# Sink-window attention and MLP: probabilities transposed on VectorE and by DMAs through DRAM instead of on TensorE, from the third chunk on

## The chip, the core and the metric

The kernel runs on one core of a Trainium2 chip. The metric is the device time of one execution in microseconds (us); of several runs the median is taken. TensorE (PE in the profile) multiplies and transposes into PSUM, VectorE (DVE), ScalarE (ACT) and GpSimd (POOL) compute elementwise, and SyncE (SP) issues the DMAs. All engines run their own queues in order and wait for each other through semaphores.

## The reference

```python
B, H, S, D = 4, 8, 768, 64          # n_sink 4, window 128
scores = (q @ k.T) / sqrt(D)        # per batch and head
keep = (key < n_sink) | ((query - key >= 0) & (query - key < window))
a = softmax(where(keep, scores, -1e9))
x = (a @ v)                         # heads side by side: 3072 x 512
h = maximum(x @ w_in, 0)            # 512 -> 2048
out = (h * h) @ w_out               # 2048 -> 512
```

A query sees the 4 sink keys and the 128 keys up to its own position. All numbers are fp32; the weights, x, and the squares are carried as a high and a low part, so that a product is three matmuls.

## The kernel before

The 3072 tokens are cut into 8 chunks of 384 tokens (half a sequence of one batch; chunk c = 2b + half), and attention for a chunk runs over 4 pairs of heads (p). Queries go in blocks of 128: three per chunk and head. A query block needs at most its own key block and the one before it, and the sinks. Its row of probabilities in P is 264 wide: the earlier key block (columns 0 to 127), 8 sink columns (128 to 135), its own key block (136 to 263). The first block of a sequence (qb = 0) has 128 columns only.

One pair goes through these steps:
- load_qk and load_v (L171, L188) load qn, kn, vn on SP's queue. prep (L211) splits keys and queries into parts KS and QS on DVE, POOL and ACT.
- score (L231): two matmuls into a PSUM bank s of the tag "att" (two banks, shared with pss and pt); DVE adds the mask and takes the minimum (L259); ACT takes the exponential and the sum (L262). After a head's third score normalise (L266) runs: rs and its reciprocal on DVE (L272, L273); POOL adds the two key blocks into columns 0 to 127 (L279), scales (L284), and writes the sink columns to PSK (L290, L293).
- probs_of (L344), once for each head: three TensorE transposes of the added blocks into a bank pt (L353), and DVE multiplies by the 0/1 masks halves that separate the two key blocks again, into PTF (L359, L362, L364). The added blocks hold both: with a window of 128, the earlier block has values above the diagonal only, the own block on and below it.
- sink_keys (L295): transposes PSK into pss (L300) and copies it to SK (L302).
- values (L368): matmuls of vn with PTF and of VS with SK into xo (L384, L387). ACT and DVE split xo into the high and low part of x (L395, L396).

The MLP runs in legs: half of the 2048 hidden features for chunks 0, 1, 0, 1, then all 16 blocks of 128 for each of chunks 2 to 7. One block is 12 matmuls into ph (L442), a ReLU r and a square gh on ACT (L450, L453), the low part gl on DVE (L455, L459), and one block later nine matmuls into the three banks po, one for each block of 128 tokens (L472). At a leg's end evacuate (L484) moves po out through ob (two buffers); for the second half of chunks 0 and 1 it loads the earlier part back (L490) and adds it (L491).

What sets the order: chunks 0 and 1 are written out by hand. From chunk 2 on, a list of units is made for each pair (slot, L415: loads, six scores, the four units of the pair before, two preps), and a plan (L717) spreads the units of the coming chunk evenly over the steps of a leg; within that the tile scheduler orders each engine's queue. The attention of chunk 2 runs beside the MLP of chunks 0 and 1, that of chunk 3 beside chunk 2, and so on; the last leg (chunk 7) has no attention beside it. During the first legs the weights are also loaded (raw, half) and split.

## Time and profile before

| | |
|---|---|
| runs | 718.26, 719.05, 719.45 us, median 719.05 |
| span of the profiled execution | 717.5 us (1.55 below the median) |
| TensorE | 691.0 us, 3866 matmuls and transposes |
| DVE, ACT, POOL | 485.7, 392.4, 232.0 us |
| DMA | 71.78 MB, hardware queue 33.5% of 16 engines |

The span is from the first to the last instruction of the profiled execution. Busy times of different engines overlap; the one near the span is the one whose queue matters. The groups of instructions list busy time, the mean duration of one in ns, and the engine's idle time ahead of them with what ended it. Matmuls follow each other in a pipeline, so that one lasts longer than it holds up the next.

### The profile page before, as it was taken

The page shows a single profiled execution, that of the slowest core. Times are in us where ns is not written, and L with a number is a line of the kernel's source. Part 1 is how long each engine was busy: PE and PEld are TensorE (multiplying, and loading weights), DVE is VectorE, ACT ScalarE, POOL GpSimd, SP SyncE. Part 2 cuts the span into 40 slices and gives each one's busy share as a digit, 9 for nine tenths or more (in the row PEclk, how much of TensorE's full clock was granted, in tenths as well). Part 3 has the DMA queues.
Part 4 walks back from the last instruction along what each step waited for, and adds up shares of the span by engine and source line. Part 5 has one row for each costly group of instructions (what it writes and reads, how often), then busy time and mean ns, then how long its engine had stood idle before and what let it go on. Part 6 is the DMA issues. An engine that isn't in the chain of part 4 may idle for free.

```text
span 717.5 us, 11750 instructions
## 1 busy us (share of the span) xinstructions
PE 691.0 (96%) x3866; PEld 597.4 (83%) x3866; DVE 485.7 (68%) x1278; ACT 392.4 (55%) x1074; POOL 232.0 (32%) x432
## 2 busy tenths in 40 slices
PE   4879999999999999999999999999999999999996
PEld 2557789998878888888988888898888898889995
DVE  6887879996887776666576766766666766543222
ACT  5677666663545665666665665666566444322221
POOL 4552420042454443333244334423342424110000
PEclk9999999999999999999999999999999999999998
DMA  8465356531433522343433433334333310001001
GB/s 238 133 203 167 110 151 211 173 106 46 140 91 80 171 77 73 105 133 94 112 102 90 134 106 93 92 116 122 84 87 103 101 44 15 1 2 45 1 0 49
DMA packets 37013, 71.78 MB, mean 100 GB/s; under 512 B 4368, under 2 KB 14096, under 8 KB 36944
## 3 DMA queue, kind: packets, MB, share of 16 engines
q1 hardware_dynamic: 36944, 70.95, 33.5%
q8 instruction: 33, 0.54, 0.3%
q14 instruction: 36, 0.29, 0.2%
HBM read 63.06 MB, written 7.86 MB: 99 GB/s over the span
## 4 chain that ended last, share of the span: by engine, by line
PE 87%; DVE 6%; POOL 2%; ACT 1%; issue 1%; DMA 1%; SPq 0%; DVEq 0%; POOLq 0%; ACTq 0%
PE ph L442 35%; PE po L472 35%; PE xo L384 5%; PE s L255 4%; PE pt L353 2%; POOL P L284 1%; PE xo L387 1%; PE pss L300 1%; PE pt L335 1%; PE s L251 1%; DVE P L259 1%; ACT P L262 1%; DMA kn<-in_k_dram 1%; DVE ph L455 0%; DVE rs L272 0%
## 5 line engine op out<-in xcount | busy, mean ns | idle before, releaser
L442 PE MATMUL ph<-x,wi 128*128 128x384 f32 x1536 | 307.8, 341 | 0.0
L442 PEld LDWEIGHTS ph<-x,wi 128*128 128x128 f32 x1536 | 265.9, 188 | 8.2 <-issue 1.7
L472 PE MATMUL po<-wo,gh 128*128 128x512 f32 x768 | 243.9, 398 | 0.5 <-DVE ob L491 0.5
L223 POOL TENSOR_TENSOR KS<-kn,KS 128x408 fp32r<-128x408 f32 (+1 forms) x48 | 71.3, 1486 | 325.3 <-DVE KS L222 315.1
L472 PE MATMUL po<-wo,gl 128*128 128x512 f32 x384 | 151.4, 394 | 0.0
L472 PEld LDWEIGHTS po<-wo,gh 128*128 128x128 f32 x768 | 135.8, 188 | 18.6 <-DVE ob L491 0.8
L262 ACT ACTIVATE P<-P,nbs 128x264 f32<-128x264 f32 (+1 forms) x192 | 94.4, 492 | 85.6 <-DVE nbs L259 82.0
L450 ACT ACTIVATE r<-ph 128x384 f32<-128x384 f32 x128 | 62.7, 490 | 109.9 <-PE ph L442 109.0
L455 DVE TENSOR_TENSOR ph<-ph,r 128x384 f32<-128x384 f32 x128 | 71.6, 560 | 66.0 <-ACT r L450 65.3
L284 POOL TENSOR_SCALAR P<-P,rs 128x136 f32<-128x136 f32 (+2 forms) x192 | 82.0, 443 | 43.9 <-DVE rs L273 33.6
L472 PEld LDWEIGHTS po<-wo,gl 128*128 128x128 f32 x384 | 72.0, 188 | 16.0
L259 DVE CUSTOM_DVE_ANT_0 P<-s,maskA 128x264 f32<-128x264 f32 x128 | 53.8, 429 | 45.9 <-PE s L255 43.8
L459 DVE TENSOR_TENSOR gl<-ph,gh 128x384 fp32r<-128x384 f32 x128 | 71.0, 555 | 10.2 <-DVE ph L455 0.5
L453 ACT ACTIVATE gh<-r 128x384 fp32r<-128x384 f32 x128 | 67.1, 524 | 3.5
L255 PE MATMUL s<-KS,QS 128*128 128x264 f32 (+1 forms) x288 | 57.2, 281 | 0.9 <-DVE nbs L259 0.8
L255 PEld LDWEIGHTS s<-KS,QS 128*128 128x128 f32 x288 | 51.7, 188 | 6.6 <-DVE nbs L259 2.2
L359 DVE TENSOR_TENSOR PTF<-pt,halves 128x256 f32<-128x256 f32 x96 | 36.2, 419 | 22.9 <-PE pt L353 22.4
L272 DVE TENSOR_SCALAR rs<-sm 128x3 f32<-128x3 f32 (+1 forms) x56 | 47.3, 844 | 3.1 <-ACT P L262 1.9
L279 POOL TENSOR_TENSOR P<-P 128x256 f32<-128x256 f32 (+1 forms) x48 | 43.3, 902 | 16.7 <-ACT P L262 16.7
L384 PE MATMUL xo<-PTF,vn 128*64 128x256 f32 (+1 forms) x448 | 46.3, 347 | 0.7 <-ACT PTF L342 0.7
L384 PEld LDWEIGHTS xo<-PTF,vn 128*64 128x64 f32 x448 | 28.8, 139 | 21.8 <-issue 10.8
L395 ACT CAST x<-xo 128x384 fp32r<-128x384 f32 x32 | 15.3, 479 | 53.4 <-PE xo L387 53.4
(94 smaller groups left out, 659.9 us busy)
## 6 DMA issues: line engine op xcount, KB each, us to landing
raw<-in_moe_w_in_dram SPq DMA_DIRECT2D x16, 512.0 KB, 5.1
raw<-in_moe_w_out_dram SPq DMA_DIRECT2D x16, 512.0 KB, 3.6
half<-in_moe_w_in_dram SPq DMA_DIRECT2D x32, 256.0 KB, 3.2
half<-in_moe_w_out_dram SPq DMA_DIRECT2D x32, 256.0 KB, 3.2
kn<-in_k_dram SPq DMA_DIRECT2D x24, 272.0 KB, 4.2
qn<-in_q_dram SPq DMA_DIRECT2D x32, 192.0 KB, 3.2
out_dram<-ob SPq DMA_DIRECT2D x24, 256.0 KB, 2.3
kn<-in_k_dram SPq DMA_DIRECT2D x24, 204.0 KB, 3.7
```

The costliest lines, as they stand in the source:

```text
L223: nc.gpsimd.tensor_tensor(KS[:, 1, 0:nk], st["kn"][:, hh, 0:nk], f32(KS[:, 0, 0:nk]), op=ALU.subtract)
L255: nc.tensor.matmul(ps[:, 0:n], st["QS", hh][:, qcols], flat[:, a, c0 : c0 + n], start=(a == 0), stop=(a == 1))
L259: nc.vector.tensor_tensor_reduce(Pt[:, i, 0:n], ps[:, 0:n], mask[:, 0:n], -SCALE, BIG, ALU.add, ALU.min, nb)
L262: nc.scalar.activation(Pt[:, i, 0:n], Pt[:, i, 0:n], AF.Exp, bias=nb, scale=-1.0, accum_out=sm[:, i : i + 1])
L284: nc.gpsimd.tensor_scalar(Pt[:, j, 0:n], Pt[:, j, 0:n], rs[:, hh, j : j + 1], 1.0, op0=ALU.mult, op1=ALU.mult)
L384: nc.tensor.matmul(xo[h * D : h * D + D, cols], lhsT, rhs, start=(n == 0), stop=False, skip_group_check=True)
L442: nc.tensor.matmul(ph[:, 0:TOK], wi_at(i, cc, fc), xt[:, cc, :], start=(m == 0), stop=(m == 3 * NCC - 1),)
L450: nc.scalar.activation(r, ph[:, 0:TOK], AF.Relu)
L453: nc.scalar.activation(gh, r, AF.Square)
L455: nc.vector.tensor_tensor(ph[:, 0:TOK], ph[:, 0:TOK], r, op=ALU.mult)
L459: late = lambda: nc.vector.tensor_tensor(gl, ph[:, 0:TOK], f32(gh), op=ALU.subtract)
L472: nc.tensor.matmul(po[t], gt[:, ts_], wo[f][:, i, :], start=(f == f0 and j == 0), stop=(f == f1 - 1 and j == 2),)
```

## The change

From chunk 2 on, TensorE's transposes of P, the masks halves and POOL's addition are gone. The function turn takes their place: DVE transposes P in blocks of 32x32 into a tile T, once both heads are done four DMAs copy T to a DRAM buffer via, one for each group of 32 partitions, and one DMA loads it back as PT, with the blocks at their transposed places. All key blocks are kept apart, so each query block has two blocks in PT: index i for its own key block (or NQ + i - 1 for the earlier one), and P of qb = 0 is stored at column 136. POOL now scales all 264 columns. values takes its moving operand from PT in four runs of 32 for each 128 columns. P, T and PT have one buffer each (P0 and P1 for the two heads). In slot, the units of the pair before are two, sink_keys behind the first score and values behind the fifth. Before, the third DVE multiply of probs_of stood for the block that only one query block uses; in turn, the third transpose (128x4x32) is issued for the second half of a sequence only.

```diff
@@ -236,7 +226,12 @@
                 st["P"] = []
                 st["sm"] = ap2.tile([P, 2, NQ], F32, tag="sm", name=f"sm_{c}_{p}")
             if i == 0:
-                st["P"].append(ap4.tile([P, NQ, BAND], F32, tag="P", name=f"P_{c}_{p}_{hh}"))
+                if c < 2 and p % 2:
+                    if hh == 0:
+                        both = ap1.tile([P, 2, NQ, BAND], F32, tag="T", name=f"P_{c}_{p}")
+                        st["P"] = [both[:, 0], both[:, 1]]
+                else:
+                    st["P"].append(ap1.tile([P, NQ, BAND], F32, tag=f"P{hh}", name=f"P_{c}_{p}_{hh}"))
             Pt, sm = st["P"][hh], st["sm"][:, hh]
             qb = half * NQ + i
             if qb == 0:
@@ -256,12 +251,16 @@
                         ps[:, 0:n], st["QS", hh][:, qcols], flat[:, a, c0 : c0 + n], start=(a == 0), stop=(a == 1)
                     )
             nb = nbs[:, c * H + 2 * p + hh, i : i + 1]
+            o = BS if c > 1 and qb == 0 else 0
             nc.vector.tensor_tensor_reduce(
-                Pt[:, i, 0:n], ps[:, 0:n], mask[:, 0:n], -SCALE, BIG, ALU.add, ALU.min, nb
+                Pt[:, i, o : o + n], ps[:, 0:n], mask[:, 0:n], -SCALE, BIG, ALU.add, ALU.min, nb
             )
-            nc.scalar.activation(Pt[:, i, 0:n], Pt[:, i, 0:n], AF.Exp, bias=nb, scale=-1.0, accum_out=sm[:, i : i + 1])
+            nc.scalar.activation(
+                Pt[:, i, o : o + n], Pt[:, i, o : o + n], AF.Exp, bias=nb, scale=-1.0, accum_out=sm[:, i : i + 1]
+            )
             if i == NQ - 1 and c * NPAIR + p >= NPS:
                 normalise(c, p, (hh,))
+                turn(c, p, hh)
 
         def normalise(c, p, heads):
             st = state[c, p]
@@ -274,15 +273,11 @@
             for hh in heads:
                 Pt = st["P"][hh]
                 j0 = 1 if half == 0 else 0
-                if c > 1:
-
-                    nc.gpsimd.tensor_tensor(
-                        Pt[:, j0:NQ, 0:P], Pt[:, j0:NQ, 0:P], Pt[:, j0:NQ, BS:BAND], op=ALU.add
-                    )
                 for j in range(NQ):
-                    n = P if j < j0 else (BS if c > 1 else BAND)
+                    n = P if j < j0 else BAND
+                    o = BS if c > 1 and j < j0 else 0
                     nc.gpsimd.tensor_scalar(
-                        Pt[:, j, 0:n], Pt[:, j, 0:n], rs[:, hh, j : j + 1], 1.0, op0=ALU.mult, op1=ALU.mult
+                        Pt[:, j, o : o + n], Pt[:, j, o : o + n], rs[:, hh, j : j + 1], 1.0, op0=ALU.mult, op1=ALU.mult
                     )
                 own = slice(hh * NS, hh * NS + NS)
                 src = Pt[:, i0:NQ, P:BS]
@@ -335,35 +330,43 @@
                     nc.tensor.transpose(
                         pt[:, off + j * P : off + (j + 1) * P], st["P"][hh][:, i, c0 : c0 + P], ident
                     )
-            st["PT"][bi] = PTF = ap3.tile([P, 512], F32, tag="PTF", name=f"PTF_{c}_{p}_{bi}")
+            st["PT"][bi] = PTF = PT.rearrange("p r i h b -> p (r i h b)")[:, bi * 512 : bi * 512 + 512]
             if bi == 1 and c != 1:
                 nc.vector.tensor_copy(PTF[:, 0:used], pt[:, 0:used])
             else:
                 nc.scalar.copy(PTF[:, 0:used], pt[:, 0:used])
 
-        def probs_of(c, p, hh):
+        def turn(c, p, hh):
 
             st = state[c, p]
-            half = c % NHALF
+            j0 = 1 if c % NHALF == 0 else 0
+            Pt = st["P"][hh]
             if hh == 0:
-                st["banks"] = banks_of(c, p)
-                st["PT"] = [ap3.tile([P, 512], F32, tag="PTF", name=f"PTF_{c}_{p}_{bi}") for bi in range(3)]
-            pt = ps_att.tile([P, 512], F32, tag="att", name=f"pt_{c}_{p}_{hh}")
-            for i in range(NQ):
-                nc.tensor.transpose(pt[:, i * P : (i + 1) * P], st["P"][hh][:, i, 0:P], ident)
-            both = lambda t, n: t.rearrange("p (a c) -> p a c", c=n)
-
-            wide = st["PT"][2 * hh].rearrange("p (a t c) -> p a t c", a=2, t=2)
-            for a in range(2):
-                m = halves[:, 0:2] if half == 0 and a == 0 else halves[:, 2:4]
-                nc.vector.tensor_tensor(wide[:, a], both(pt[:, a * P : (a + 2) * P], P), m, op=ALU.mult)
-            thin = both(st["PT"][1], P)
-            if half == 0:
-                nc.vector.tensor_tensor(thin[:, hh], pt[:, 2 * P : 3 * P], halves[:, 2], op=ALU.mult)
-            else:
-                nc.vector.tensor_tensor(
-                    thin[:, hh : 4 : 2], both(pt[:, 0 : 4 * P], P)[:, 0:4:2], halves[:, 1:3], op=ALU.mult
+                st["T"] = ap1.tile([P, 4, 2 * NQ, 2, 32], F32, tag="T", name=f"T_{c}_{p}")
+            T = st["T"]
+            nc.vector.transpose(
+                T[:, :, 0:NQ, hh].rearrange("p c j b -> p j c b"),
+                Pt[:, :, BS:BAND].rearrange("p j (c b) -> p j c b", b=32),
+            )
+            nc.vector.transpose(
+                T[:, :, NQ : 2 * NQ - 1, hh].rearrange("p c j b -> p j c b"),
+                Pt[:, 1:NQ, 0:P].rearrange("p j (c b) -> p j c b", b=32),
+            )
+            if j0 == 0:
+                nc.vector.transpose(T[:, :, 2 * NQ - 1, hh], Pt[:, 0, 0:P].rearrange("p (c b) -> p c b", b=32))
+            if hh == 0:
+                return
+            used = slice(0, 2 * NQ - j0)
+            via = dp.tile([4, 32, 4, 2 * NQ, 2, 32], F32, tag=f"via{p % 2}", name=f"via_{c}_{p}")
+            for r in range(4):
+                nc.sync.dma_start(
+                    out=via[:, :, r, used].rearrange("c a i h b -> a c (i h b)"),
+                    in_=T[32 * r : 32 * r + 32, :, used].rearrange("a c i h b -> a c (i h b)"),
                 )
+            nc.sync.dma_start(
+                out=PT[:, :, used].rearrange("p r i h b -> p r (i h b)"),
+                in_=via[:, :, :, used].rearrange("c a r i h b -> (c a) r (i h b)"),
+            )
 
         def values(c, p, later=False):
 
@@ -373,10 +376,25 @@
             xo = ps_x.tile([P, 512], F32, tag="xo", name=f"xo_{c}_{p}")
             todo = ([], [])
 
-            for bi in (0, 2, 1):
-                for h, kk, qs, off in st["banks"][bi][0]:
-                    n = len(qs) * P
-                    todo[h].append((slice(qs[0] * P, qs[0] * P + n), st["vn"][:, kk, h, :], st["PT"][bi][:, off : off + n]))
+            if c > 1:
+                half = c % NHALF
+                for h in range(2):
+                    blocks = PT[:, :, :, h].rearrange("p r i b -> p i r b")
+                    for kk in sorted(range(st["nk"]), key=lambda kk: kk in (half - 1, half + 2)):
+                        j = kk - half
+                        if j < 0:
+                            idx, cols = slice(2 * NQ - 1, 2 * NQ), slice(0, P)
+                        elif j == NQ - 1:
+                            idx, cols = slice(j, j + 1), slice(j * P, j * P + P)
+                        else:
+                            idx, cols = slice(j, j + NQ + 1, NQ), slice(j * P, j * P + 2 * P)
+                        todo[h].append((cols, st["vn"][:, kk, h, :], blocks[:, idx]))
+            else:
+                for bi in (0, 2, 1):
+                    for h, kk, qs, off in st["banks"][bi][0]:
+                        n = len(qs) * P
+                        cols = slice(qs[0] * P, qs[0] * P + n)
+                        todo[h].append((cols, st["vn"][:, kk, h, :], st["PT"][bi][:, off : off + n]))
             with tc.manual_schedule(engines={mybir.EngineType.PE}) if c > 1 else nullcontext():
                 for n in range(len(todo[0])):
                     for h in (1, 0):
@@ -407,19 +425,17 @@
 
 
         def values_of(a):
-            return [
-                lambda: probs_of(*a, 0), lambda: probs_of(*a, 1), lambda: sink_keys(*a), lambda: values(*a),
-            ]
+            return [lambda: sink_keys(*a), lambda: values(*a)]
 
 
         def slot(s):
 
             c, p = pairs[s]
             sc = [lambda h=h, i=i: score(c, p, h, i) for h in range(2) for i in range(NQ)]
-            va = values_of(pairs[s - 1]) if s > PAUSE else [lambda: None] * 4
+            va = values_of(pairs[s - 1]) if s > PAUSE else [lambda: None] * 2
             units = [
-                lambda: start_pair(s + 1), sc[0], va[0], sc[1], va[1], va[2], sc[2], lambda: prep(s + 1, 0),
-                va[3], sc[3], sc[4], sc[5], lambda: prep(s + 1, 1),
+                lambda: start_pair(s + 1), sc[0], va[0], sc[1], sc[2], lambda: prep(s + 1, 0),
+                sc[3], sc[4], va[1], sc[5], lambda: prep(s + 1, 1),
             ]
             if p == 0 and c % NHALF == 0:
                 units.append(lambda: load_sinks(c // NHALF)())
@@ -483,8 +499,10 @@
 
         def evacuate(c, f0, f1, po):
             for t in range(NQ):
-                pool, tag = (ap3, "PTF") if c == NCHUNK - 1 and t == 2 else (mp, "ob")
-                ob = pool.tile([P, DM], F32, tag=tag, name=f"ob_{c}_{f0}_{t}")
+                if c == NCHUNK - 1 and t == 2:
+                    ob = PT.rearrange("p r i h b -> p (r i h b)")[:, 0:DM]
+                else:
+                    ob = mp.tile([P, DM], F32, tag="ob", name=f"ob_{c}_{f0}_{t}")
                 r0 = c * TOK + t * P
                 if f0 > 0:
                     nc.sync.dma_start(out=ob, in_=part[c, t])
```

In parts left out, the pools ap3 and ap4 and the tile halves are removed, and PT is allocated among the fixed tiles.

The new order at three places. Names end in numbers of their own in each kernel; in the names of chunk tiles the first number after the letters is the pair, then the head and the query block (s_1_0_2), or the feature block and token block (po_0_1).

TensorE, first scores of pair 1 of chunk 6 beside the first blocks of chunk 5's MLP, before:

```order
L255 MATMUL s_1_0_0_5671<-KS_1_0_5504,QS_1_0_5505 128x128 x2
L353 MATMUL pt_0_0_5679<-ident,P_0_0_5400 128x128 x3
L442 MATMUL ph_0_5655<-x_5_4810,wi 128x384
L255 MATMUL s_1_0_1_5686<-KS_1_0_5504,QS_1_0_5505 128x264 x2
L442 MATMUL ph_0_5655<-x_5_4810,wi 128x384
L442 MATMUL ph_0_5655<-x_5_4811,wi 128x384
L442 MATMUL ph_0_5655<-x_5_4810,wi 128x384 x2
L442 MATMUL ph_0_5655<-x_5_4811,wi 128x384
L353 MATMUL pt_0_1_5702<-ident,P_0_1_5543 128x128 x3
```

and now:

```order
L250 MATMUL s_1_0_0_5530<-KS_1_0_5340,QS_1_0_5341 128x128 x2
L295 MATMUL pss_0_5535<-ident,PSK 128x128 x2
L458 MATMUL ph_0_5514<-x_5_4701,wi 128x384 x2
L250 MATMUL s_1_0_1_5539<-KS_1_0_5340,QS_1_0_5341 128x264 x2
L458 MATMUL ph_0_5514<-x_5_4702,wi 128x384
L458 MATMUL ph_0_5514<-x_5_4701,wi 128x384 x2
L458 MATMUL ph_0_5514<-x_5_4702,wi 128x384
```

The six transposes into pt are gone, and the sink transposes pss stand right behind the first score instead of behind the second head's transposes.

TensorE, the same slot from the third score on, before:

```order
L255 MATMUL s_1_0_2_5745<-KS_1_0_5504,QS_1_0_5505 128x264 x2
L442 MATMUL ph_1_5738<-x_5_4810,wi 128x384 x2
L442 MATMUL ph_1_5738<-x_5_4811,wi 128x384
L442 MATMUL ph_1_5738<-x_5_4810,wi 128x384 x2
L442 MATMUL ph_1_5738<-x_5_4811,wi 128x384
L472 MATMUL po_0_0_5777<-wo_488,gh_0_5699 128x512 x2
L472 MATMUL po_0_0_5777<-wo_488,gl_0_5700 128x512
L472 MATMUL po_0_1_5778<-wo_488,gh_0_5699 128x512 x2
L472 MATMUL po_0_1_5778<-wo_488,gl_0_5700 128x512
L384 MATMUL xo_0_5786<-PTF_0_2_5678,vn_0_5386 64x256
L384 MATMUL xo_0_5786<-PTF_0_0_5676,vn_0_5386 64x256
L384 MATMUL xo_0_5786<-PTF_0_2_5678,vn_0_5386 64x256
```

and now, from the fifth score on:

```order
L250 MATMUL s_1_1_1_5636<-KS_1_1_5454,QS_1_1_5455 128x264 x2
L458 MATMUL ph_2_5650<-x_5_4701,wi 128x384 x2
L458 MATMUL ph_2_5650<-x_5_4702,wi 128x384
L458 MATMUL ph_2_5650<-x_5_4701,wi 128x384 x2
L458 MATMUL ph_2_5650<-x_5_4702,wi 128x384
L458 MATMUL ph_2_5650<-x_5_4701,wi 128x384 x2
L458 MATMUL ph_2_5650<-x_5_4702,wi 128x384
L458 MATMUL ph_2_5650<-x_5_4701,wi 128x384 x2
L402 MATMUL xo_0_5657<-PT,vn_0_5246 64x256 x4
L402 MATMUL xo_0_5657<-PT,vn_0_5246 64x128 x2
L405 MATMUL xo_0_5657<-SK,VS 128x256
L458 MATMUL ph_2_5650<-x_5_4702,wi 128x384
```

xo of pair 0 stood between the third and the fourth score of pair 1; it stands between the fifth and the sixth now, and reads PT.

DVE, at the end of the second leg of chunk 1, where the parts of chunk 1 are added into ob, before:

```order
L359 TENSOR_TENSOR PTF_0_0_2719<-pt_0_0_2722,halves 128x256 x2
L364 TENSOR_TENSOR PTF_0_1_2720<-pt_0_0_2722,halves 128x2x128
L259 ISA P_1_0_2713,nbs<-s_1_0_1_2729,maskA 128x264
L259 ISA nbs 128x1
L455 TENSOR_TENSOR ph_0_2698<-ph_0_2698,r_0_2740 128x384
L359 TENSOR_TENSOR PTF_0_2_2721<-pt_0_1_2745,halves 128x256 x2
L364 TENSOR_TENSOR PTF_0_1_2720<-pt_0_1_2745,halves 128x2x128
L459 TENSOR_TENSOR gl_0_2743<-ph_0_2698,gh_0_2742 128x384
L491 TENSOR_TENSOR ob_8_0_2763<-po_8_0_2235,ob_8_0_2763 128x512
L491 TENSOR_TENSOR ob_8_1_2767<-po_8_1_2236,ob_8_1_2767 128x512
L302 CAST SK<-pss_0_2780 128x384
L259 ISA P_1_0_2713,nbs<-s_1_0_2_2792,maskA 128x264
```

and now:

```order
L272 RECIPROCAL rs_1_1_2820<-rs_1_1_2820 128x3
L347 STREAM_TRANSPOSE T_1_2701<-P_1_0_2654 128x3x4x32
L351 STREAM_TRANSPOSE T_1_2701<-P_1_0_2654 128x2x4x32
L356 STREAM_TRANSPOSE T_1_2701<-P_1_0_2654 128x4x32
L347 STREAM_TRANSPOSE T_1_2701<-P_1_1_2739 128x3x4x32
L215 TENSOR_TENSOR QS_2_0_2727<-qn_2_2646,QS_2_0_2727 64x384
L351 STREAM_TRANSPOSE T_1_2701<-P_1_1_2739 128x2x4x32
L356 STREAM_TRANSPOSE T_1_2701<-P_1_1_2739 128x4x32
L215 TENSOR_TENSOR QS_2_1_2845<-qn_2_2646,QS_2_1_2845 64x384
L212 CAST KS_2_0_2726<-kn_2_2647 128x544
L212 CAST KS_2_1_2844<-kn_2_2647 128x544
L509 TENSOR_TENSOR ob_8_0_2709<-po_8_0_2218,ob_8_0_2709 128x512
```

The addition ob_8_0 stood behind the mask multiplies of pair 0 of chunk 3; it stands behind the transposes of pair 1, two QS and two KS now.

More of the change, by code (lines that the diff above doesn't have):

```diff
@@ L70, in sink_window_attention_moe @@
         mp = fast.enter_context(tc.tile_pool(name="mp", bufs=2))
-        ap3 = fast.enter_context(tc.tile_pool(name="ap3", bufs=3))
         ap2 = fast.enter_context(tc.tile_pool(name="ap2", bufs=2))
-        ap4 = fast.enter_context(tc.tile_pool(name="ap4", bufs=4))
         ps_att = fast.enter_context(tc.tile_pool(name="ps_att", bufs=2, space=PSUM))
@@ L139, in sink_window_attention_moe @@
         wo = {}
+        PT = wp.tile([P, 4, 2 * NQ, 2, 32], F32, name="PT")
         wchk = wp.tile([P, 2, 2 * (NCC * NFQ + NFC)], F32, name="wchk")
@@ L155, in sink_window_attention_moe @@
             nc.gpsimd.memset(f32(t), 0.0)
-        halves = wp.tile([P, 4, P], F32, name="halves")
-        nc.gpsimd.memset(halves, 1.0)
-        for t in (1, 3):
-            nc.gpsimd.affine_select(
-                halves[:, t], halves[:, t], pattern=[[-1, P]], compare_op=ALU.is_gt, fill=0.0, base=0, channel_multiplier=1
-            )
-        nc.gpsimd.affine_select(
-            halves[:, 2], halves[:, 2], pattern=[[1, P]], compare_op=ALU.is_ge, fill=0.0, base=0, channel_multiplier=-1
-        )
         nbs = wp.tile([P, NCHUNK * H, NQ], F32, name="nbs")
@@ L276, in normalise @@
                 j0 = 1 if half == 0 else 0
-                if c > 1:
-                    nc.gpsimd.tensor_tensor(
-                        Pt[:, j0:NQ, 0:P], Pt[:, j0:NQ, 0:P], Pt[:, j0:NQ, BS:BAND], op=ALU.add
-                    )
                 for j in range(NQ):
-                    n = P if j < j0 else (BS if c > 1 else BAND)
+                    n = P if j < j0 else BAND
+                    o = BS if c > 1 and j < j0 else 0
                     nc.gpsimd.tensor_scalar(
-                        Pt[:, j, 0:n], Pt[:, j, 0:n], rs[:, hh, j : j + 1], 1.0, op0=ALU.mult, op1=ALU.mult
+                        Pt[:, j, o : o + n], Pt[:, j, o : o + n], rs[:, hh, j : j + 1], 1.0, op0=ALU.mult, op1=ALU.mult
                     )
```

## The prediction

> **What bounds the kernel now.** I read the page from the top: the engines' shares, the slices, the chain that ended last. Then the windows by stage, TensorE's waits, and the timeline around one group of transposes.
>
> ```profile
> span 717.5 us, 11750 instructions
> PE 691.0 (96%) x3866; PEld 597.4 (83%) x3866; DVE 485.7 (68%) x1278; ACT 392.4 (55%) x1074; POOL 232.0 (32%) x432
> PEclk9999999999999999999999999999999999999998
> PE 87%; DVE 6%; POOL 2%; ACT 1%; issue 1%; DMA 1%; SPq 0%; DVEq 0%; POOLq 0%; ACTq 0%
> ```
>
> TensorE is busy 96% of the span, at nearly its full granted clock in every slice, and holds 87% of the chain that ended last. Work taken from TensorE shortens the span as long as nothing else makes it wait.
>
> Columns of the next view: window, its length, then busy time and count of each engine, granted clock, DMA share, GB/s.
>
> ```profile
> 180.00:200.00 20.00, 19.35 (x113) 16.29 (x112) 16.68 (x51) 10.65 (x31) 10.74 (x21) 1.00 0.45 135
> 200.00:220.00 20.00, 18.50 (x112) 15.26 (x112) 16.08 (x44) 8.97 (x26) 9.11 (x15) 1.00 0.30 75
> 300.00:400.00 100.00, 100.00 (x566) 88.57 (x565) 65.71 (x177) 62.97 (x192) 34.22 (x64) 1.00 0.38 108
> ```
>
> There are two regimes. From 220 us to about 637 us TensorE never stops, and DVE has a third of its time free (65.7 of 100). Around chunk 2, 180 to 220 us, TensorE already idles 0.65 + 1.50 = 2.15 us and DVE is busy 16 to 17 us of 20: two legs' ends, the last weight rows and attention units one behind the other. From 140 to 640 us TensorE's listed waits are these three:
>
> ```profile
> PE s L255 <- DVE nbs L259: 0.8, 1, 0.8
> PE pt L353 <- DVE PTF L362: 0.7, 1, 0.7
> PE po L472 <- DVE ob L491: 0.5, 1, 0.5
> ```
>
> So outside that stage there is no wait to win back. The change gives what it takes from TensorE's queue, less the waits that it puts in.
>
> **What is removed from TensorE.** For 24 head pairs, 6 transposes each go.
>
> ```profile
> 433.54 0.62 PE L472 MATMUL po<-wo,gh 128*128 128x512 f32 x2
> 434.00 0.39 PE L472 MATMUL po<-wo,gl 128*128 128x512 f32 x1
> 434.22 0.49 PE L353 MATMUL pt<-ident,P 128*128 128x128 f32 x3
> 434.47 0.71 PE L472 MATMUL po<-wo,gh 128*128 128x512 f32 x2
> 435.02 0.39 PE L472 MATMUL po<-wo,gl 128*128 128x512 f32 x1
> L353 PE MATMUL pt<-ident,P 128*128 128x128 f32 x144 | 23.6, 273 | 0.7 <-DVE PTF L362 0.7
> ```
>
> Matmuls overlap, so I don't take the 273 ns. From the start of the gh pair to the start of the gl that follows is 434.00 - 433.54 = 0.46 us without transposes; from gl to gl with three between is 435.02 - 434.00 = 1.02, of which the gl itself takes 434.22 - 434.00 = 0.22 and the gh pair 0.46. The three cost 0.34 us. 48 groups x 0.34 = **16.3 us**, the ceiling of the gain. (144 x 273 ns would be 39 us, the group's busy time is 23.6; both count time in which the neighbours run.)
>
> **What is removed from DVE and POOL, and what comes.**
>
> ```profile
> L359 DVE TENSOR_TENSOR PTF<-pt,halves 128x256 f32<-128x256 f32 x96 | 36.2, 419 | 22.9 <-PE pt L353 22.4
> L222 DVE CAST KS<-kn 128x408 fp32r<-128x408 f32 x24 | 8.8, 367 | 0.0
> L272 DVE TENSOR_SCALAR rs<-sm 128x3 f32<-128x3 f32 x48 | 45.9, 957 | 2.8 <-ACT P L262 1.6
> L284 POOL TENSOR_SCALAR P<-P,rs 128x264 f32<-128x264 f32 x40 | 26.2, 667 | 22.3 <-DVE rs L273 18.7 <-ACT m L533 3.6
> 188.98 1.36 POOL L223 TENSOR_TENSOR KS<-kn,KS 128x408 fp32r<-128x408 f32 x1 [4.31 <-DVE KS L222]
> 190.31 0.73 POOL L279 TENSOR_TENSOR P<-P 128x256 f32<-128x256 f32 x1
> 191.29 1.08 POOL L284 TENSOR_SCALAR P<-P,rs 128x128 f32<-128x128 f32 x3 [0.26 <-DVE rs L273]
> 192.43 0.21 POOL L290 CAST PSK<-P 128x32 fp32r<-128x32 f32 x1
> 192.73 0.22 POOL L293 TENSOR_TENSOR PSK<-P,PSK 128x16 fp32r<-128x16 f32 x1
> ```
>
> No row shows DVE's transpose of 32x32 blocks. The cast L222 moves 408 elements per partition in 367 ns, 0.9 ns each; a two-input operation, L359, takes 419 ns for 256, 1.6 ns each. 640 elements (first half of a sequence) or 768 (second) per head then cost 0.58 to 1.26 us; I take 0.65 to 0.8, by the cast, since the operand is one tile in SBUF as there. Before, a head's multiplies were 2 x 0.42 + 0.28 to 0.42. DVE's load stays about even and it is not the bound; its place in the queue matters, below. POOL loses the add (0.73 here) and its three scalings go from 128 or 136 to 264 wide: 3 x 0.36 = 1.08 becomes between 1.3 (by width, half of it fixed) and 2.0 (667 ns, a mean that holds waits). I take 1.4. POOL's chain for one head gets 0.4 us shorter.
>
> The xo matmuls stay the same in number and columns, but their moving operand is read in runs of 32 elements.
>
> ```profile
> L384 PE MATMUL xo<-PTF,vn 128*64 128x256 f32 x256 | 35.8, 402 | 0.7 <-ACT PTF L342 0.7
> ```
>
> No strided moving operand is in the trace. Bounds: nothing (or a few tenths below it), and a doubling of the pipelined cost, at most 24 x 1.4 us = 33 us. I take nothing, since the runs are whole 128-byte pieces.
>
> **The round trip, and whether TensorE waits for it.** The last score of a pair must become PT before xo of that pair. Quoted: the last score of one slot, then xo in its old place, then the next slot's fifth score, behind which xo stands now; then the DMAs.
>
> ```profile
> 449.18 0.41 PE L255 MATMUL s<-KS,QS 128*128 128x264 f32 x2
> 463.72 1.52 PE L384 MATMUL xo<-PTF,vn 128*64 128x256 f32 x16
> 468.79 0.41 PE L255 MATMUL s<-KS,QS 128*128 128x264 f32 x2
> out_dram<-ob SPq DMA_DIRECT2D x24, 256.0 KB, 2.3
> qn<-in_q_dram SPq DMA_DIRECT2D x32, 192.0 KB, 3.2
> kn<-in_k_dram SPq DMA_DIRECT2D x24, 272.0 KB, 4.2
> raw<-in_moe_w_in_dram SPq DMA_DIRECT2D x16, 512.0 KB, 5.1
> kn<-in_k_dram SPq DMA_DIRECT2D x8, 136.0 KB, 5.4
> 431.43 0.61 SPq L183 DMA_DIRECT2D kn<-in_k_dram  x1
> ```
>
> Distance: 468.79 - 449.18 = 19.6, less the 0.68 of transposes gone from it, about 19 us; counted through the new order at TensorE's pace the slots give 17.2 (last pair of a chunk) to 22.3. Length: reduce 0.5 and exponential 0.7, then rs 0.96, reciprocal 0.2, scalings 1.4, transposes 0.7, with 2.3 to 3 for what stands between them on DVE and POOL (a key cast, QS, the x rest, the low part of KS with 1.36): 6.8 to 7.5. Four copies out to DRAM, 160 or 192 KB each: issues 4 x 0.61 (the two-dimensional kn issue) and 2.3 for the last to land, 4.7. The load of PT, 640 or 768 KB: between qn's 3.2 and raw's 5.1, taken as 4.2. **16 to 17 us against 19**: hidden, with 1 to 3 us to spare, least at the last pair of a chunk. If this cover goes, TensorE loses the whole difference in every slot. The vn and kn loads behind PT in SP's queue have most of a slot before they are needed.
>
> A rule would lengthen it: the Trainium skill, SBUF — State Buffer, section "Door 1: The DMA port swizzle", says that 32 consecutive partitions reach 8 of 16 ports at about 27 GB/s each; by that four copies of 192 KB need 3.6 us of transfer (an estimate from the page) where I count issues and landing alone. The 64-partition kn loads reach as few by that rule, and 272 KB of them land 1.0 us after 192 KB of qn would: the trace doesn't decide it.
>
> **The crowded stage.** From chunk 2 to the second pair of chunk 3 the order puts units closer together, and in the new one I find these waits on TensorE, each worked out along the queues.
> ```profile
> 436.55 1.20 PE L442 MATMUL ph<-x,wi 128*128 128x384 f32 x6
> 437.59 0.49 PE L353 MATMUL pt<-ident,P 128*128 128x128 f32 x3
> L259 DVE CUSTOM_DVE_ANT_0 P<-s,maskA 128x264 f32<-128x264 f32 x128 | 53.8, 429 | 45.9 <-PE s L255 43.8
> L262 ACT ACTIVATE P<-P,nbs 128x264 f32<-128x264 f32 x160 | 81.6, 510 | 53.8 <-DVE nbs L259 52.2 <-POOL P L284 1.0
> L491 DVE TENSOR_TENSOR ob<-po,ob 128x512 f32<-128x512 f32 x6 | 4.0, 685 | 0.1
> ```
>
> Six ph matmuls take 437.59 - 436.55 = 1.04 us, a po one 0.23 (0.46 for the gh pair above). A reduce is 0.43 and an exponential 0.51, with the reading of their accumulators 0.5 and 0.7.
>
> - pss of pairs 1 and 2 of chunk 2 stands 2.9 us of work (six ph, six po, a score) behind the last score; the sink rows come after reduce 0.5, cast 0.37 and POOL's 1.36 + 1.4 + 0.43 with the rs and hops between, 5.3: 2 x 2.4 = 4.8.
> - Scores in a row without filler, each waiting for a bank until the reduce two before it is done: three, then five at the leg's change, 3.
> - po of tokens 2 behind the add of part (DVE, below both heads' transposes): 1.8.
> - Casts of KS just ahead of their scores: 1.2. x copy after the chunk's last xo: 0.7.
> - At the change from chunk 1 to chunk 2's leg, po_0_0 waits for the add ob_8_0, which DVE has behind six transposes, two QS and two KS casts: 7.9 + 0.3 of hops after the last score, with 4.3 of TensorE work in between (twelve ph 2.08, xo 1.45, a score and pss): 4 (the load of ob behind PT adds up to 0.8).
> - po_0_2 waits for the add ob_8_2, behind rs and reciprocal of the pair whose last score stands right before it: reduce 0.5, exponential 0.7, rs 0.96, reciprocal 0.2, add 0.69 = 3.
>
> In all 18.5 to 19.3. A wait lets the engines behind catch up, so later ones shrink; I count 13, less the 2.15 that this stage has already: **+11**. Each of the other four chunk ends has x copies (ACT, then DVE) after the last xo with little filler: 0.5 each, **+2**.
>
> **Sum.** 717.5 - 16.3 + 11 + 2 = 714.2 us of span. The profiled execution's span lies 1.55 below the runs' median of 719.05; with it the time is **716**, 0.4% faster. About 0.2% (1.4 us) is what a measurement of this kernel can tell from no change. Its own range, with a third to all of the 19 counted: 6 - 2 gives 709, 19 - 2 gives 722.
>
> **Rivals.**
> - *The crowded stage costs next to nothing* (chance 0.25). For: DVE has 3 to 4 us of 20 free there now, and idle time of TensorE lets it catch up. Against: adds behind six transposes are new. 717.5 - 16.3 + 2 to 5 + 1 + 1.55 = 706 to 709.
> - *The round trip is longer than its distance* (0.20), slower. For: three queued transfers where one step was, only 1 to 3 us of cover; small kn loads took 5.4. Against: writes landed in 2.3. It decides from 18 us on. At 7.5 + 2.4 + 5.4 + 5.1 + 0.3 = 20.7 the steady slots lose nearly 2 us each, 20 x 1.9 = 38: 754. At 1 us short 736. By the Trainium skill's 8 ports alone it would be 17 to 18.5, 0 to 8 us in all: up to 724.
> - *xo is slower by its short runs* (0.07): half of the bound, 16 us, 732.
> - *DVE, waiting for POOL before each head's transposes, holds up the ph and gl that TensorE needs* (0.08): 24 x 0.2 to 0.5 more, 721 to 728. Against: TensorE is 2 us ahead of gl in a steady slot.
> - That the transposes don't vanish is excluded by the order.
>
> **Chances.** The forecast has 0.40, of it 0.24 below 717.6, 0.08 within 0.2%, 0.08 above. Faster 0.24 + 0.25 = 0.49; same 0.08 + 0.04 (half of DVE's case) = 0.12; slower 0.08 + 0.20 + 0.07 + 0.04 = 0.39. Cases of both signs hold much; the likeliest's own range is 709 to 722. The wide one, 704 to 738, leaves out the far end of the first rival (0.04), half of the round trip's (0.10) and half of xo's (0.04).
>
> **What will show it.** Right: pt gone from the page; TensorE at 100% from 300 to 600 us, no wait of xo for PT there; idle time of 8 to 20 us between 160 and 260 us, for PSK, ob and nbs. Copies out landing in 2 to 3 us and PT in 4 to 5. Wrong: xo waiting for PT in each slot (round trip); xo's 402 ns grown; TensorE waiting for gl all along (DVE). The place where I am least sure is the length of the three transfers.

## The result, and the profile after

The changed kernel took **731.33 us** (median of 4 runs, 729.48 to 732.18) against 719.25 of the kernel before beside it: ratio 1.0167, 95% interval 1.0142 to 1.0193. Forecast was 716, 0.4% faster; it is 1.7% slower. The profiled execution's span went from 717.5 to 727.7 us.

The page of the changed kernel (span, busy time of each engine, TensorE's busy share in 40 slices of 18.2 us, the chain that ended last):

```profile
span 727.7 us, 11498 instructions
PE 682.4 (94%) x3722; PEld 585.1 (80%) x3722; DVE 456.3 (63%) x1254; ACT 388.0 (53%) x1074; POOL 193.7 (27%) x380
PE   4789999989889789999999999999999999999996
PE 79%; DVE 8%; POOL 4%; ACT 3%; DMA 2%; issue 2%; SPq 0%; POOLq 0%; DVEq 0%; ACTq 0%
```

and TensorE's slices of the kernel before, 17.9 us each:

```profile
PE   4879999999999999999999999999999999999996
```

TensorE is busy 8.6 us less, not 16.3, and its share of the chain fell from 87% to 79%. Between 145 and 273 us five slices show less than a 9, where the kernel before had nines throughout. To see how much, I cut both spans at the first ph matmul of each leg. Windows of the kernel before, for the second halves of chunks 0 and 1, then the legs of chunks 2 and 4:

```profile
139.00:175.30 36.30, 36.30 (x195) 33.06 (x194) 32.40 (x82) 19.88 (x47) 12.37 (x19) 1.00 0.29 92
175.30:226.00 50.70, 48.55 (x288) 40.83 (x287) 38.61 (x113) 24.36 (x69) 25.10 (x47) 1.00 0.34 93
226.00:309.90 83.90, 83.90 (x490) 74.00 (x489) 59.71 (x152) 50.89 (x155) 34.29 (x62) 1.00 0.37 107
392.50:476.40 83.90, 83.90 (x490) 74.08 (x489) 58.01 (x149) 52.20 (x158) 32.59 (x59) 1.00 0.37 108
```

and of the changed kernel, the same legs:

```profile
138.70:180.80 42.10, 39.38 (x206) 34.71 (x205) 33.07 (x86) 21.64 (x52) 10.03 (x18) 0.96 0.38 113
180.80:229.30 48.50, 43.10 (x240) 37.09 (x239) 31.20 (x98) 22.01 (x63) 19.23 (x40) 1.00 0.57 157
229.30:324.40 95.10, 88.19 (x479) 75.40 (x478) 56.88 (x158) 49.55 (x154) 28.01 (x50) 0.96 0.59 172
405.80:488.60 82.80, 81.79 (x466) 71.92 (x465) 52.69 (x147) 47.67 (x146) 24.67 (x48) 1.00 0.60 174
```

The three legs of the crowded stage went from 170.9 to 185.7 us, **+14.8**. All that follows, from the first ph of chunk 3's leg to the end, went from 717.5 - 309.9 = 407.6 to 727.7 - 324.4 = 403.3, **-4.3**. The part before them is even within 0.3. In the three legs TensorE idles 2.72 + 5.40 + 6.91 = 15.0 us, where it was 2.15.

TensorE's waits of the changed kernel from 140 to 650 us:

```profile
PE pss L295 <- POOL PSK L288: 4.1, 3, 2.0
PE po L488 <- DVE gl L475: 3.0, 2, 2.7
PE po L488 <- DVE ob L513: 2.4, 2, 1.4
PE po L488 <- DVE ob L509: 2.2, 1, 2.2
PE s L250 <- POOL KS L213: 1.9, 2, 1.1
PE s L250 <- DVE KS L212: 1.7, 1, 1.7
PE s L250 <- DVE nbs L255: 1.5, 4, 0.5
PE ph L458 <- DVE gl L475: 1.0, 1, 1.0
```

No xo waits for PT. How the longest one, for gl, comes about (timeline of the changed kernel):

```profile
157.07 1.43 POOL L213 TENSOR_TENSOR KS<-kn,KS 128x408 fp32r<-128x408 f32 x1 [4.00 <-DVE KS L212]
159.38 1.45 POOL L279 TENSOR_SCALAR P<-P,rs 128x128 f32<-128x128 f32 x3 [0.88 <-DVE rs L272]
160.86 0.58 DVE L347 STREAM_TRANSPOSE T<-P 128x384 f32<-128x384 f32 x1 [0.83 <-POOL P L279]
161.36 0.40 DVE L351 STREAM_TRANSPOSE T<-P 128x256 f32<-128x256 f32 x1
161.69 0.52 DVE L475 TENSOR_TENSOR gl<-ph,gh 128x384 fp32r<-128x384 f32 x1
162.26 0.80 PE L488 MATMUL po<-wo,gl 128*128 128x512 f32 x1 [2.72 <-DVE gl L475]
```

DVE stands at the transpose until POOL has scaled, and gl, which needed nothing of this, stands behind it: TensorE idles 2.72 us. The price goes on. Windows of 3.41 us, TensorE alone: the first holds that idle time, the third idle time at the change of legs, and the second and fourth stand right behind each:

```profile
158.48:161.89 3.41, 1.06 (x6) 1.00 0.55 140
161.89:165.31 3.42, 3.05 (x8) 0.52 0.91 218
257.47:260.88 3.41, 1.23 (x5) 1.00 0.02 5
260.88:264.29 3.41, 3.41 (x10) 0.52 0.96 266
```

TensorE then runs at half the clock for 3.41 us, a loss of up to 1.7 each time; a third such window starts at 250.6 us. Together some 5.1 us that my sum did not have. This agrees with what the Trainium skill, TensorE: Matmul & The Clock Gate, "Part 1: The HAM clock gate (the "warmup" mystery)" says of the window (3413 ns) and of the two clocks. Where its table speaks of an idle window, a window 64% idle sufficed here.

### The profile page after: what moved, and what is told of

Read it like the earlier page. It is cut to its first block, busy times and chain, and to the rows that moved or that the text cites. A ratio compares the mean times of both kernels' runs of the same rounds, so it can differ in the third digit from the quotient of the medians.

```text
span 727.7 us, 11498 instructions
## 1 busy us (share of the span) xinstructions
PE 682.4 (94%) x3722; PEld 585.1 (80%) x3722; DVE 456.3 (63%) x1254; ACT 388.0 (53%) x1074; POOL 193.7 (27%) x380
## 4 chain that ended last, share of the span: by engine, by line
PE 79%; DVE 8%; POOL 4%; ACT 3%; DMA 2%; issue 2%; SPq 0%; POOLq 0%; DVEq 0%; ACTq 0%
PE po L488 33%; PE ph L458 32%; PE xo L402 5%; PE s L250 4%; POOL P L279 2%; DVE P L255 1%; PE xo L405 1%; ACT P L258 1%; PE pss L295 1%; PE s L246 1%; PE pt L330 1%; DMA vn<-in_v_dram 1%; DMA raw<-in_moe_w_in_dram 1%; DVE gl L475 1%; DVE rs L271 1%
## 5 line engine op out<-in xcount | busy, mean ns | idle before, releaser
L458 PE MATMUL ph<-x,wi 128*128 128x384 f32 x1536 | 302.8, 339 | 1.6 <-DVE gl L475 1.0
L488 PEld LDWEIGHTS po<-wo,gh 128*128 128x128 f32 x768 | 139.1, 191 | 26.8 <-DVE ob L513 3.3
L279 POOL TENSOR_SCALAR P<-P,rs 128x264 f32<-128x264 f32 (+1 forms) x192 | 95.7, 515 | 202.1 <-DVE rs L272 145.5
L213 POOL TENSOR_TENSOR KS<-kn,KS 128x408 fp32r<-128x408 f32 (+1 forms) x48 | 64.5, 1348 | 229.5 <-DVE KS L212 210.3
L402 PE MATMUL xo<-PT,vn 128*64 128x256 f32 (+1 forms) x448 | 46.7, 349 | 0.9 <-ACT PT L337 0.9
L347 DVE STREAM_TRANSPOSE T<-P 128x384 f32<-128x384 f32 x48 | 27.6, 576 | 31.1 <-POOL P L279 28.8
L402 PEld LDWEIGHTS xo<-PT,vn 128*64 128x64 f32 x448 | 28.9, 140 | 21.0 <-issue 9.8
L258 ACT ACTIVATION_READ_ACCUMULATOR P<-P,nbs 128x1 f32 x192 | 35.9, 187 | 0.0
L585 ACT ACTIVATE sq<-sq,theta 128x256 bf16<-128x256 bf16 x64 | 32.3, 505 | 1.3
```

The costliest lines, as they stand in the source:

```text
L213: nc.gpsimd.tensor_tensor(KS[:, 1, 0:nk], st["kn"][:, hh, 0:nk], f32(KS[:, 0, 0:nk]), op=ALU.subtract)
L258: nc.scalar.activation(Pt[:, i, o : o + n], Pt[:, i, o : o + n], AF.Exp, bias=nb, scale=-1.0, accum_out=sm[:, i : i + 1])
L279: nc.gpsimd.tensor_scalar(Pt[:, j, o : o + n], Pt[:, j, o : o + n], rs[:, hh, j : j + 1], 1.0, op0=ALU.mult, op1=ALU.mult)
L402: nc.tensor.matmul(xo[h * D : h * D + D, cols], lhsT, rhs, start=(n == 0), stop=False, skip_group_check=True)
L458: nc.tensor.matmul(ph[:, 0:TOK], wi_at(i, cc, fc), xt[:, cc, :], start=(m == 0), stop=(m == 3 * NCC - 1),)
L488: nc.tensor.matmul(po[t], gt[:, ts_], wo[f][:, i, :], start=(f == f0 and j == 0), stop=(f == f1 - 1 and j == 2),)
```

## The experiments

All are compared with the kernel before run beside them (719.0 to 720.2 us); the intervals are 95%.

**e1, the new path for chunks 4 to 7 alone** (chunks 2 and 3 as before, with the old units and masks). Two places of its edit:

```diff
-            o = BS if c > 1 and qb == 0 else 0
+            o = BS if c > 3 and qb == 0 else 0
...
-                turn(c, p, hh)
+                if c > 3:
+                    turn(c, p, hh)
```

> The new path for chunks 4 to 7 alone; chunks 2 and 3 keep the transposes on TensorE. Theory (the loss is waits, and the half clock behind them, in the crowded stage where chunk 2 and the first pairs of chunk 3 are worked on, 139 to 262 us): that stage goes back to its time of before, the later four chunks keep 2.7 us each less about 1 us for waits at each leg's end: 719 - 11 + 4 = 712 us, 708 to 715. Rival (DMA traffic and the round trip cost time everywhere): half of the loss stays, 724 to 727 us.

Measured 714.56 us, ratio 0.9948 (0.993 to 0.9966): the change is a gain where TensorE bounds, and the loss sits in the crowded stage.

**e2, fewer units in the first leg of that stage.** (A leg (0, 8, 16) is chunk 0 with its feature blocks 8 to 15.)

```diff
-(ready[1] + 24, 24, NROW, 0.9)
+(ready[1] + 20, 24, NROW, 0.9)
```

> Only the number of units of chunk 2 that the plan puts beside the leg (0, 8, 16) goes from 24 to 20: a pair has 11 units now where it had 13, so 24 units are 2.0 pairs where they were 1.6. Theory (crowded stage): that leg's 42.1 us come down by 2 to 4 us, part of it comes back in the next leg: 727 to 730 us. Rival (the order in the stage doesn't matter, DMA does): 731 us, no change.

735.13 us, ratio 1.0237: the wrong way. The first leg came down from 42.1 to 37.7 us, as expected, and the second went from 48.5 to 56.9. Moving the units only moves the crowd.

**e3, the ceiling.** The first lines of its edit:

```diff
-            pt = ps_att.tile([P, 512], F32, tag="att", name=f"pt_{c}_{p}_{hh}")
-            for i in range(NQ):
-                nc.tensor.transpose(pt[:, i * P : (i + 1) * P], st["P"][hh][:, i, 0:P], ident)
+            Pt = st["P"][hh]
```

> The kernel before without TensorE's 144 transposes of the added blocks: the mask multiplies read P itself, so x is not the attention's. Measures the ceiling of the change's gain: by my 0.34 us for three 719 - 16 = 703 us; if three cost only 0.22 us, 708 us.

709.69 us, ratio 0.9889 (0.9864 to 0.9914), 9 us and not 16. Its windows for the three legs of the stage and for chunk 4's leg:

```profile
139.50:175.60 36.10, 36.00 (x189) 32.47 (x188) 32.39 (x82) 19.91 (x47) 13.27 (x19) 1.00 0.30 92
175.60:228.00 52.40, 46.41 (x270) 38.91 (x269) 40.44 (x115) 24.08 (x69) 25.40 (x46) 1.00 0.32 89
228.00:310.90 82.90, 81.51 (x466) 71.82 (x465) 61.26 (x155) 50.67 (x155) 34.96 (x63) 1.00 0.38 108
390.70:471.90 81.20, 81.20 (x466) 71.70 (x465) 61.37 (x152) 51.50 (x158) 32.84 (x59) 1.00 0.38 110
```

In chunk 4's leg 8 groups of three transposes are worth 83.9 - 81.2 = 2.7 us, 0.34 each, exactly my price. In the crowded stage the same removal is worth nothing: 36.1 + 52.4 + 82.9 = 171.4 against 170.9. Busy time fell there by 4.8 us, and the idle time grew by 5.3: TensorE did not set the pace.

**e4, no copies** to DRAM and back: xo reads T, which takes turns with PT as its second buffer.

```diff
-                st["T"] = ap1.tile([P, 4, 2 * NQ, 2, 32], F32, tag="T", name=f"T_{c}_{p}")
+                st["T"] = PT if p % 2 else ap1.tile([P, 4, 2 * NQ, 2, 32], F32, tag="T", name=f"T_{c}_{p}")
...
-                    blocks = PT[:, :, :, h].rearrange("p r i b -> p i r b")
+                    blocks = st["T"][:, :, :, h].rearrange("p r i b -> p i r b")
```

> The changed kernel without the copies to DRAM and back: xo reads T, which has two buffers in turn (T and PT); the 32x32 blocks stay at their untransposed places, so x is not the attention's. Theory (DVE's and POOL's queues in the crowded stage): the waits stay, 724 to 731 us. Rival (DMA traffic, late ob and kn loads, the round trip): the loss goes, 706 to 716 us.

722.37 us, ratio 1.0055 (1.0036 to 1.0074): between the two. The copies carry 9 us of the 22 that lie between the change and the ceiling; chunk 2's leg falls from 95.1 to 86.2. The first leg stays at 43.6. (The profiled execution took 726.46 us, the slowest of the five.)

**e5, the new path from chunk 3 on** (as e1, with c > 2).

> The new path from chunk 3 on; chunk 2 alone keeps TensorE's transposes. In the changed kernel the legs (0,8,16) and (1,8,16), beside which chunk 2's attention runs, cost 3.7 us more than before, and the leg of chunk 2, beside which chunk 3's runs, 11.1 us more. If chunk 3's start at the change of legs carries the larger part by itself, 722 to 728 us; if it was only pushed into trouble by chunk 2, about 713 us.

719.12 us, ratio 0.9985 (0.9967 to 1.0003), between the two expectations. Chunk 2's leg has 89.8 us: chunk 3's start makes half of its 11 us extra alone.

**e6, sink_keys behind the third score.**

```diff
-                lambda: start_pair(s + 1), sc[0], va[0], sc[1], sc[2], lambda: prep(s + 1, 0),
+                lambda: start_pair(s + 1), sc[0], sc[1], sc[2], va[0], lambda: prep(s + 1, 0),
```

> The changed kernel with the unit sink_keys behind the third score instead of the first. Theory (waits of TensorE for the sink rows, 4.1 us listed for pss, and the half clock that idle time brings): 725 to 728 us. Rival (the wait only moves to the next instruction): 731 us.

772.99 us, ratio 1.0739: my edit was a mistake, but a telling one. Behind the third score the next pair's normalise has already written PSK, so pss waits for that pair's scalings (and by the code the first head's sink rows are then the next pair's). The waits of this run:

```profile
PE pss L295 <- POOL PSK L288: 36.3, 24, 3.8
```

These 24 waits, 36.3 us against 4.1 in the changed kernel, and five windows at half clock more (eight from 140 to 700 us, against three; some 1.7 us each) make 40.7 of the 41.7 us that it is behind the changed kernel. It says nothing on where the sinks should stand.

**e7, no transposes on DVE**: the DMAs copy P itself.

```diff
-                    in_=T[32 * r : 32 * r + 32, :, used].rearrange("a c i h b -> a c (i h b)"),
+                    in_=T[32 * r : 32 * r + 32],
...
+            T = st["both"].rearrange("p h j n -> p (h j n)")[:, 0 : 4 * n].rearrange("p (c n) -> p c n", n=n)
```

> The changed kernel without DVE's transposes: the DMAs copy P itself, of the same size and shape, so x is not the attention's; a POOL memset of 136 columns for each head of a first half is added. Theory A (DVE standing at the transposes holds up what TensorE waits for): the crowded stage gives back 10 us or more, 714 to 721 us. Theory B (DMA and SP's queue): 727 to 731 us.

721.94 us, ratio 1.0028 (1.0009 to 1.0047), just outside theory A's range. The three legs take 38.9, 48.0 and 92.3 us, 6.5 less than in the changed kernel, where theory A asked for 10 or more and B for nothing. Half of that is the first leg's, as by theory A; chunk 2's leg keeps most of its excess, for which the copies are left (e4).

**e8, late transposes**, xo behind the sixth score.

```diff
-                turn(c, p, hh)
...
-            return [lambda: sink_keys(*a), lambda: values(*a)]
+            return [lambda: sink_keys(*a), lambda: turn(*a, 1), lambda: values(*a)]
...
-                lambda: start_pair(s + 1), sc[0], va[0], sc[1], sc[2], lambda: prep(s + 1, 0),
-                sc[3], sc[4], va[1], sc[5], lambda: prep(s + 1, 1),
+                lambda: start_pair(s + 1), sc[0], va[0], va[1], sc[1], sc[2], lambda: prep(s + 1, 0),
+                sc[3], sc[4], lambda: turn(c, p, 0), sc[5], va[2], lambda: prep(s + 1, 1),
```

> The changed kernel with the transposes as units of their own: the first head's behind the fifth score, the second head's behind the next pair's first score, and xo behind the sixth. Theory A: DVE no longer waits for POOL at them, 720 to 727 us. Theory B (order isn't the matter): 731 us; if the round trip then is too long for its distance, more, 735 to 745 us.

720.09 us, ratio 1.0012 (0.9989 to 1.0035). The same instructions in another order give back 11 us, 5.5 of them in the first leg and some 2 in the last two. At the place shown above, its timeline has

```profile
159.80 0.55 DVE L474 TENSOR_TENSOR gl<-ph,gh 128x384 fp32r<-128x384 f32 x1
164.61 0.58 DVE L346 STREAM_TRANSPOSE T<-P 128x384 f32<-128x384 f32 x1 [0.64 <-POOL P L278]
```

DVE still waits 0.64 us for POOL, but gl is ahead, and the first leg is back at 36.6 us. Chunk 2's leg keeps 93.9.

**e9, e8 and e4 together.**

> The late transposes of e8 together with the missing copies of e4 (x is not the attention's). If order and copies cost time apart from each other, 731 - 11 - 9 = 711 us; if both lose it to the same thing, the work bunched where two legs meet, 718 to 721 us.

709.23 us, ratio 0.9853 (0.9822 to 0.9884): at the ceiling of e3. With e4 and e8 this is a table of two by two: 731.3 and 720.1 with copies, 722.4 and 709.2 without; order costs 11 to 13, the copies 9 to 11, nearly independent of each other. Its three legs take 36.7, 49.9 and 83.3 us, 169.9 together, where the kernel before has 170.9: the whole loss of the crowded stage is gone. P still has one buffer for each head here, so that the fewer buffers of P are not the cause.

**e10, all the traffic, but nobody waits for it.** To e4 are added the four copies out and one from via to a DRAM buffer in place of the load of PT.

> The changed kernel with all its DMA traffic and places in SP's queue, but nobody waits for it: T goes out to via, via is copied to another DRAM buffer of the same size in place of PT, and xo reads T, which has two buffers as in e4 (x is not the attention's). If traffic and SP's queue carry the 9 us that e4 gave back, 729 to 733 us; if it is the latency of the round trip, which xo has to wait out, 721 to 724 us.

733.75 us, ratio 1.0199 (1.0164 to 1.0233). It isn't the latency that xo waits out; it is what the five DMAs do in SP's queue or on the DMA engines. T has two buffers here as in e4, so it isn't T's single buffer either.

**e11, the parts loaded two blocks ahead of the leg's end.**

```diff
+                if f0 > 0 and f == f1 - 2:
...
+                    for t in range(NQ):
+                        nc.sync.dma_start(out=early[c][t], in_=part[c, t])
```

> The changed kernel with the three parts of a chunk loaded two feature blocks ahead of the leg's end, the third into a tile of its own. If late loads of ob make the order at the change of legs what it is, the leg of chunk 2 loses 5 us or more: 722 to 726 us. If not (the last xo of the chunk comes late there), 729 to 733 us.

721.41 us, ratio 1.0026 (1.001 to 1.0043), 10 us back. SyncE's queue shows where the loads of chunk 1's parts stand, in the kernel before (the first of these three is still chunk 0's):

```profile
187.71 0.96 SPq L490 DMA_DIRECT2D ob<-part  x2
193.21 0.32 SPq L490 DMA_DIRECT2D ob<-part  x1
```

and in the changed kernel (other loads in between left out):

```profile
231.41 2.25 SPq L362 DMA_DIRECT2D via<-T  x4
238.69 0.46 SPq L366 DMA_DIRECT2D PT<-via  x1
240.47 0.91 SPq L508 DMA_DIRECT2D ob<-part  x2
247.80 0.32 SPq L362 DMA_DIRECT2D via<-T  x1
249.81 1.40 SPq L518 DMA_DIRECT2D out_dram<-ob  x2
251.26 0.42 SPq L362 DMA_DIRECT2D via<-T  x1
251.84 0.35 SPq L508 DMA_DIRECT2D ob<-part  x1
```

Before, the first two parts went out 33 to 38 us ahead of chunk 2's leg, which starts at 226.0 us. Here that leg starts at 229.3, and they stand behind a pair's copies and go out 11 us into it. SP then stands 6 us at the next copy, which waits for the last transpose. This is what followed on DVE and TensorE:

```profile
249.10 0.68 DVE L509 TENSOR_TENSOR ob<-po,ob 128x512 f32<-128x512 f32 x1
259.37 0.68 DVE L509 TENSOR_TENSOR ob<-po,ob 128x512 f32<-128x512 f32 x1
260.10 0.73 PE L488 MATMUL po<-wo,gh 128*128 128x512 f32 x2 [2.18 <-DVE ob L509]
```

The three adds come 20, 21 and 30 us into the leg; in the kernel before it was 6, 6 and 12, without the copies (e4) 6, 8 and 14, in e11 17 to 19. Their parts had landed 3 to 4 us earlier, so what held the adds at the end was their place in DVE's queue, behind transposes and casts, and the outputs and the third part's load waited for the first adds (249.10 + 0.68 = 249.78, outputs at 249.81). That the adds got this place because the loads come late is an inference. e11 also gives the third part a tile of its own; the loads' time and that tile weren't tried apart.

**e12, chunks 4 to 7 with late transposes** (e1 and e8).

> Chunks 4 to 7 alone on the new path, with the late transposes of e8: a version that should beat both. From e1 (714.6 us) the last two legs give back the 2.2 us that they did in e8: 711 to 714 us.

**711.85 us, ratio 0.9884 (0.9853 to 0.9914): 1.2% faster than before**, the fastest version that computes the whole attention.

**e13, both repairs on all chunks from 2 on** (e8 and e11), and **e14, the control for e11**: e4 with the early loads.

> The changed kernel with both repairs, late transposes (e8) and early loads of the parts (e11), all chunks from 2 on, nothing left out. If these are the two separate causes, 731 - 11 - 10 = 710 us, at the ceiling of e3 and e9, and the fastest correct version. If both repair the same stretch, 718 to 720 us.

717.88 us, ratio 0.9979 (0.996 to 0.9998): the repairs don't add up as e9 does.

> Control for e11: the early loads of the parts in the kernel without the copies (e4, 722.4 us; x is not the attention's). If the early loads only undo what the copies in SP's queue did, 721 to 724 us; if they are a gain of their own, 711 to 714 us.

722.0 us, ratio 1.0037 (1.0024 to 1.005): without copies the early loads (with the third tile) are worth nothing, so e11 repairs what the copies did.

## Why the prediction was wrong

Two steps failed. The gain was counted in full where TensorE already waited: 16.3 us forecast, 717.5 - 707.3 = 10.2 by e3. And the copies were priced by their latency, which was hidden, with 0.8 us for all else: they cost 9 to 11 by e4, e8 and e9. The cost of order, 11 to 13 us by the same runs, is what I had with 11 + 2, in part by luck.

**What bounds, and the gain.** "Work taken from TensorE shortens the span as long as nothing else makes it wait" was right, and I had read in the same windows that from 180 to 220 us others already made it wait, DVE busy 16 to 17 us of 20. Still I counted 0.34 us for all 48 groups. e3 shows 2.7 us a leg where TensorE bounds and nothing for the 16 groups of chunks 2 and 3: 16.3 should have been about 11.

**The crowded stage.** The place was right, and the waits for KS and pss behind DVE's work, and the idle time came close: +12.9 measured, +11 forecast. That closeness is partly luck. Of the 15.0 us idle in the three legs 4.0 are waits for gl, which were not in my list; 2.2 are a wait for an add into ob, where I had 1.8 + 4 + 3 = 8.8; KS has 3.6 where I had 1.2. My sum made these three legs 11 - 5.4 = 5.6 us longer (5.4 is the share of the 16 groups in the 16.3); they are 14.8 longer. Of the 9.2 us between, some 5.1 are the three windows at half clock, since I had priced idle time at its own length only; 1.9 are idle time beyond the 11; the other 2.2, busy time of TensorE, I can't assign. The single largest wait, 2.7 us for gl, was my rival of the gl that stands behind the transposes (0.08); I had put it in steady slots and excluded it by TensorE's lead there, and it happened where there is no lead. e8 shows that this is order, not work.

**The copies.** I costed them as a round trip with a distance. As far as it went, that was right:

```profile
458.97 0.40 PE L250 MATMUL s<-KS,QS 128*128 128x264 f32 x2
464.82 1.41 SPq L362 DMA_DIRECT2D via<-T  x3
470.30 0.33 SPq L366 DMA_DIRECT2D PT<-via  x1
479.98 1.52 PE L402 MATMUL xo<-PT,vn 128*64 128x256 f32 x16
via<-T SPq DMA_DIRECT2D x48, 192.0 KB, 3.3
PT<-via SPq DMA_DIRECT2D x12, 768.0 KB, 5.6
```

From the last score to the landing of PT: 470.30 + 5.6 - 458.97 = 17 us by the median landing (forecast 16 to 17), 18 for this pair, whose load took 6.8; xo 21 us behind. Each transfer is 1 to 1.4 us longer than I took. Over the 24 pairs PT landed 1.9 to 9.8 us ahead of its xo, and the rival of the longer round trip fell. But the transfers hold SP's queue, and what stands behind them there I had waved off for kn and vn ("most of a slot before they are needed") and given 0.8 us for ob; e4 and e9 put 9 to 11 us on the copies, e10 shows that it isn't the latency, and e11 with e14 that early loads of ob repair it.

**The other terms.** Transposes on DVE: 576 + 404 ns a head, and 272 ns more in the second half of a sequence, 0.98 to 1.25 us where I had 0.65 to 0.8; DVE's load did stay even or less. xo's strided operand cost nothing: its rows have 404 ns against 402. The chunk ends and the last pair: from chunk 3's leg on e3 takes 707.3 - 310.9 = 396.4 us, 11.2 less than the kernel before (I had 32 groups x 0.34 = 10.9), and the changed kernel 403.3, so that ends and last pair cost 6.9 where I had 2: 3.5 in the legs of chunks 3 to 5, 3.4 in the last two, where the last pair's xo now falls into the last leg (653.5 us, the leg starts at 648.1) and TensorE waits 0.6 and 1.0 us behind it.

**In sum**, the span came out at 727.7 where I had 714.2. Of these 13.5 us by place, 9.2 lie in the three legs; 4.9 - 0.3 = 4.6 behind them, by the ends and the slightly larger gain; the part ahead of them is 0.3 shorter. By cause, 6.1 are gain that wasn't there (16.3 - 10.2), and 7.4 are cost above e3 (727.7 - 707.3 = 20.4) beyond the 13 of the sum.

Left open: why e13 stays 8.7 us behind e9. From 140 us on it has 5.9 us of waits for PSK, 1.7 for PT, and two windows at half clock; no run separates these. Nor does a run separate the copies' place in SP's queue from their traffic on the DMA engines. Whether another DMA queue for the copies would do what e11 did wasn't tried.

## What to carry to other kernels

Price the removal of work stage by stage: in the stage where the engine already waited it was worth nothing here (e3), and idle time put in there cost its length and the half clock behind it. An instruction that waits for a slower engine should not be queued ahead of work that a third engine needs; moving it one or two scores later, with the same instructions, was worth 1.5% here (e8). Copies that nobody waits for can still cost time: 11 us from e4 to e10. If a change pays only in the steady part, use it only there (e12).

## What the runs showed of the hardware

- TensorE needn't be idle for a whole window to fall to half clock: windows of 3.41 us with 64 to 82% idle were each followed by one at half; in e13 one with 49% was too; the window of the changed kernel from 185.78 to 189.20 us, 37% idle, was not. Over all the runs' traces, with windows cut where the granted clock changes, every full-clock window at least 56% idle was followed by half, none up to 45% was, and between 46 and 53% both happened (e13's 49%, and 49% in e9 from 209.82 to 213.23 us with the full clock behind it).
- DVE's 32x32 transposes of fp32 take 272, 404 and 576 ns for 128, 256 and 384 elements per partition: 1.0 to 1.3 ns for each more element, and some 0.14 us of fixed time (272 - 128 x 1.03 ns).
- 32-partition copies of 192 KB landed in 3.3 us, 128-partition loads of the same 768 KB in 5.6.
